# Three double bursts of attention instead of six single ones in a fused attention and feed-forward kernel

## The chip, the cores and the metric

The kernel runs on one core of one Trainium2 chip. The core has TensorE (PE in the profile; its weight loads are PEld), VectorE (DVE), ScalarE (ACT), GpSimd (POOL) and SyncE (SP), which work side by side and meet through semaphores; each carries out its own instructions in the order in which the program lists them. SP and POOL mostly issue DMAs. The metric is the device time of one execution in microseconds (us). Before the change its median over 3 runs is 819.44 us (819.32 to 822.13).

## The reference

Attention works in chunks: each row of 64 tokens of one head attends only to its own chunk. The result, laid out as 4608 tokens of 512 numbers, goes through a feed-forward pair of matrices with a quadratic relu between them. All of it is fp32.

```python
B, H, S, D = 8, 8, 576, 64
scores = (1 / sqrt(D)) * matmul(q_c, k_c.transpose(0, 1, 2, 4, 3))   # chunks of 64
scores = scores - max(scores, axis=-1, keepdims=True)
attn = exp(scores); attn = attn / (sum(attn, axis=-1, keepdims=True) + 1e-09)
x = matmul(attn, v_c)  # then to (B * S, H * D) = (4608, 512)
h = x @ w_in           # w_in (512, 2048)
g = where(h >= 1, h, where(h <= -1, 0, (h + 1) ** 2 / 4))
out = g @ w_out        # w_out (2048, 512)
```

## The kernel before

**Tiles and turns.** The 4608 tokens are nine tiles of 512 (`NTILE`). In each tile the eight heads are four pairs (`NP`), so that attention has 36 *turns*, one for each tile and pair; `turn` numbers them and `AT` gives tile and pair back. Tiles 0 to 2 (`ALONE`) are worked one at a time. Tiles 3 and 4, then 5 and 6, then 7 and 8 go together: for two tiles at once a scheme of seven block products (`P1` to `P7`, in the manner of Strassen) makes first h (the loop over `alternating(0, NQ)`, 56 products of six matmuls of 512 columns, in `product`, L903) and then the output (`both_out`, 56 products of twelve matmuls, L1119). Turns 20 to 27 are tiles 5 and 6, turns 28 to 35 tiles 7 and 8; turns of equal number modulo two share their buffers.

**A turn** is: the loads of q and k (`load_heads`, L382, four DMAs of 64 KB each, rows of 32 numbers, on SP) and of v (L398, two DMAs); two block transposes on DVE that make `qT` and `kT` (`attn_turn`, L441; one buffer of each); the scores, 32 matmuls of 64 columns (`scores_of`, L465); the softmax (`attn_softmax`: a maximum on DVE at L521, eight exponentials on ACT at L532, normalising on DVE at L550 to L556, a block transpose on DVE at L573, and eight DMAs at L565 that move the quarters into `aT`, four on SP and four on POOL); the values, 32 matmuls (`values_of`, L487); and a copy out of the bank on ACT (`keep_x`). Of `q_sb`, `k_sb`, `v_sb` and `aT` there are two buffers each. Scores and values of a turn go into the bank pair `ps_a`.

**Bursts.** While two tiles are in their h and output stages, the attention of the next two runs in between: `between` is called ahead of each product, and at the places of `BURSTS` (5, 14, 23, ... 68, counted over the 112 products of both stages) it calls `burst`, which puts on PE the values of turn n and the scores of turn n + 2 in one stretch. There are eight bursts in the stages of tiles 3 and 4 (for turns 20 to 27) and eight in those of tiles 5 and 6 (turns 28 to 35). Six of each eight lie in the h stage.

**The order.** Everything is added to a `Plan`, which writes the instructions out by a list schedule: a part goes to its engine when the plan's own costs say that it is ready, the earlier added first, with `ahead` moving a part's place. So the order on each engine is fixed when the program is built, and a change of a cost or a place can move instructions on all of them. POOL also issues the loads of the ring of ten factors (256 KB each) from which each product takes one (`from_ring`), and its share of the moves into `aT`.

**Temporaries and banks.** `tmp_bufs` are four buffers; in tiles 0 to 2 the weights are prepared and the output rows are staged in them (`store`, L671 for the DMAs of tile 2, issued on SP). From tile 3 on they are not used. The bank pair of `ps_o2` and `ps_o3` (`o_pair`) is used in the output stages and not in the h stages.

Of the kernel before, what the change touches and what calls it, by code (L numbers as in the profile page):

```python
# [133 lines left out]
def kernel(  # L134
# [38 lines left out]
    def turn(t, g):  # L173
        if t <= ALONE:
            return t * NP + g
        d, m = divmod(t - ALONE - 1, 2)
        return (ALONE + 1) * NP + d * 2 * NP + 2 * g + m

    AT = {turn(t, g): (t, g) for t in range(NTILE) for g in range(NP)}

    sb = ctx.enter_context(tc.tile_pool(name="sb", bufs=1))
# [75 lines left out]
    def room(name, bufs, t, g):  # L257
        if t == 0 and (name, g) in first:
            return first[name, g]
        if t > 0 and name in ("e", "x"):  # L260
            return wheel[(2 * turn(t, g) + (name == "x")) % 3]
        return bufs[turn(t, g) % len(bufs)]

# [208 lines left out]
    def values_of(t, g):  # L472


        akey, aT = room("aT", aT_bufs, t, g)
        vkey, v_sb = room("v", v_bufs, t, g)
        pkeys, pair = bank_pair_of(t, g)
        halves = aT.rearrange("p (e c q) -> p c e q", e=2, q=Q)

        def emit():  # L480
            for n in range(CT // 2):
                for h in range(2):
                    at = (2 * n + h) * C
                    of = h * HALF + n * C
                    for half in range(2):
                        rows = slice(half * C, (half + 1) * C)
                        nc.tensor.matmul(  # L487
                            out=pair[h * C:(h + 1) * C, half, HALF + n * C:HALF + (n + 1) * C],
                            lhsT=v_sb[rows, of:of + C],
                            rhs=aT[rows, at:at + C] if t == 0 else halves[rows, of // C],  # L490
                            start=True, stop=True,
                        )

        return emit, (f"{akey}_0", f"{akey}_1", vkey), pkeys

    def attn_products(*some, lag=0.0):

        plan.add(
            "pe", 0.2 + 0.6 * len(some), lambda: [emit() for emit, _, _ in some],
            [k for _, reads, _ in some for k in reads],  # L500
            [k for _, _, writes in some for k in writes],
            columns=1024 * len(some), lag=lag,
        )

    def bank_pair_of(t, g):
        if t == 0 and g % 2:
            return ("ps_o2", "ps_o3"), o_pair
        return ("ps_a0", "ps_a1"), a_pair

    def attn_softmax(t, g):  # L510
# [14 lines left out]
        if sums:  # L525
            plan.add("dve", 0.08, lambda: nc.vector.tensor_scalar_mul(mx, mx, -SCALE), (), (mkey,))  # L526

            many = 2 if t > ALONE else 1

# [52 lines left out]
    def attn_split(t, g):  # L582
        if t > ALONE:
            keep_x(t, g)
            return
        pkeys, pair = bank_pair_of(t, g)
        hkey, xh = xh_bufs[g][t % 2]
# [163 lines left out]
    def keep_x(t, g):  # L751
        i = g // 2
        pkeys, pair = bank_pair_of(t, g)
        name = "eo"[g % 2] + "BA"[(t - ALONE) % 2]
# [194 lines left out]
    LATER = -60  # L949
    BURSTS = range(5, 72, 9)  # L950
    sums = {
# [109 lines left out]
    def both_out(t, wide=(), then=None):  # L1061
# [123 lines left out]
        for name in OUT_ORDER:  # L1185
            taken["slots"] = 0 if name in some else taken["slots"]
            for p in range(NQ):
                between(len(alternating(0, NQ)) + NQ * OUT_ORDER.index(name) + p)
                if last and name == "P3" and p >= NQ - 2:
# [188 lines left out]

    def between(n):
        if n in BURSTS and turns:  # L1380
            burst(*turns.pop(0))

    turns = [(n, n + 2) for n in range((ALONE + 3) * NP, ALL - 2)] + [(ALL - 2, None), (ALL - 1, None)]
    for t in range(ALONE + 1, NTILE, 2):
        if t > ALONE + 1:
            move_blocks()
        for n, (p, name) in enumerate(alternating(0, NQ)):
            between(n)
            if t == ALONE + 1 and name == "P1":
# [72 lines left out]
```

## Time and profile before

| what | value |
|---|---|
| median of 3 runs | 819.44 us |
| the profiled execution | 821.0 us |
| its span, first to last instruction | 819.2 us |
| PE busy | 808.1 us (99%) |
| DVE busy | 659.2 us (80%) |
| ACT busy | 538.3 us (66%) |
| granted TensorE clock, mean of the span | 1.000 |
| DMA, moved in the span | 181.61 MB, mean 222 GB/s |

A busy PE row says that a matmul was under way, not that PE was at its peak: matmuls are pipelined, and what a product costs is best read from the distance between the starts of two products that follow each other. An instruction's own time can also overlap that of the next one on its engine. `x6` at the end of a timeline row means that six like instructions are merged into it.

### The profile page before, as it was taken

What the parts mean: (1) busy time and instruction counts of PE and PEld (TensorE: products, weight loads), DVE (VectorE), ACT (ScalarE), POOL (GpSimd) and SP (SyncE); (2) the same over time, 40 slices, a digit from 0 to 9 for tenths busy, and PEclk for the clock granted to TensorE, in tenths of its full rate; (3) what the DMA queues carried; (4) which work ended last, traced back from release to release, by engine and by line L of the source; (5) the groups of instructions that cost most, each with busy time, mean ns of one, the idle gap of its engine ahead of it and who ended that gap; (6) DMA issues with size and microseconds to landing.
All of it is one profiled execution on the core that took longest, in us unless ns stands there. A gap on an engine that the chain in (4) does not pass through costs nothing.

```text
span 819.2 us, 18533 instructions
## 1 busy us (share of the span) xinstructions
PE 808.1 (99%) x6464; PEld 694.7 (85%) x6464; DVE 659.2 (80%) x1143; ACT 538.3 (66%) x1295; POOL 343.2 (42%) x606
## 2 busy tenths in 40 slices
PE   8999999999999999999999999999999999999998
PEld 7888778878888888878899998878999988888887
DVE  4899997768799976887899875778995845589963
ACT  4799876455677675778985446878844456686450
POOL 2112223565655463546454333554433333333330
PEclk9999999999999999999999999999999999999999
DMA  9999725887998896999999678987676776667763
GB/s 205 260 266 309 176 47 142 252 276 220 285 260 231 209 276 155 299 270 285 257 244 267 183 232 245 246 232 219 193 201 183 227 220 196 192 190 192 213 200 110
DMA packets 245356, 181.61 MB, mean 222 GB/s; under 512 B 192656, under 2 KB 210576, under 8 KB 245264
## 3 DMA queue, kind: packets, MB, share of 16 engines
q0 software_dynamic: 40640, 122.72, 47.7%
q1 hardware_dynamic: 202512, 57.18, 30.6%
q8 instruction: 52, 0.85, 0.4%
q10 hardware_dynamic: 2112, 0.52, 0.3%
q14 instruction: 40, 0.33, 0.1%
HBM read 133.17 MB, written 38.80 MB: 210 GB/s over the span
## 4 chain that ended last, share of the span: by engine, by line
PE 86%; DMA 6%; DVE 3%; SPq 2%; ACT 1%; issue 1%; DVEq 0%; POOL 0%; ACTq 0%; POOLq 0%
PE ps_o L1119 19%; PE ps_h L610 14%; PE ps_o L646 13%; PE ps_h L903 13%; PE ps_o L903 13%; PE ps_h L1119 8%; PE ps_a L1119 3%; PE ps_a L487 2%; DMA words<-in_moe_w_in_dram 2%; PE ps_a L465 2%; DMA k_sb<-in_k_dram 1%; DMA aT<-e 1%; SPq L398 1%; DMA first<-in_q_dram 1%; DMA new_wo<-combos 1%
## 5 line engine op out<-in xcount | busy, mean ns | idle before, releaser
L728 ACT CAST new_wi<-new_wi 128x512 fp32r<-128x512 f32 x156 | 94.5, 625 | 63.8 <-PE ps_o L1119 32.1
L732 DVE TENSOR_TENSOR new_wi<-new_wi,new_wi 128x512 fp32r<-128x512 f32 (+2 forms) x194 | 124.8, 673 | 13.2 <-ACT new_wi L728 12.8
L610 PE MATMUL ps_h<-xh,parts 128*128 128x512 f32 x384 | 129.9, 397 | 1.7 <-DVE parts L350 1.2
L646 PE MATMUL ps_o<-parts,gh 128*128 128x512 f32 x384 | 118.4, 390 | 0.0
L610 PEld LDWEIGHTS ps_h<-xh,parts 128*128 128x128 f32 x384 | 71.9, 188 | 18.5 <-DVE parts L350 2.1
L565 POOL DMA_DIRECT2D aT<-e x96 | 48.5, 512 | 88.7 <-ACT tmp L323 34.3
L646 PEld LDWEIGHTS ps_o<-parts,gh 128*128 128x128 f32 x384 | 71.9, 188 | 15.0
L646 PE MATMUL ps_o<-parts,gl 128*128 128x512 f32 x192 | 74.7, 389 | 0.0
L934 DVE SCALAR_TENSOR_TENSOR new_wi<-h,new_wi 128x512 f32<-128x512 f32 x62 | 41.8, 685 | 30.7 <-ACT new_wi L933 30.0
L532 ACT ACTIVATE e<-ps_a,mx 128x64 f32<-128x64 f32 x168 | 50.8, 330 | 12.1 <-DVE mx L526 5.7
L933 ACT ACTIVATE new_wi<-new_wi 128x512 f32<-128x512 f32 x84 | 51.7, 639 | 0.9
L610 PE MATMUL ps_h<-x_parts,parts 128*128 128x512 f32 x128 | 50.0, 390 | 0.0
L930 ACT ACTIVATE new_wi<-h 128x512 f32<-128x512 f32 x62 | 38.9, 642 | 13.1 <-DVE h L924 12.8
L629 ACT CAST gh<-r 128x512 fp32r<-128x512 f32 x48 | 29.9, 622 | 26.6 <-DVE r L621 16.6
L646 PEld LDWEIGHTS ps_o<-parts,gl 128*128 128x128 f32 x192 | 36.0, 188 | 7.5
L621 DVE SCALAR_TENSOR_TENSOR r<-ps_h,r 128x512 f32<-128x512 f32 x48 | 32.6, 682 | 9.7 <-ACT r L620 9.7
L732 DVE TENSOR_TENSOR new_wi<-new_wi 128x512 f32<-128x512 f32 (+2 forms) x64 | 40.0, 631 | 0.5
L617 ACT ACTIVATE r<-ps_h 128x512 f32<-128x512 f32 x48 | 29.2, 608 | 14.9 <-PE ps_h L610 14.7
L532 ACT ACTIVATION_READ_ACCUMULATOR e<-ps_a,mx 128x1 f32 x168 | 37.3, 222 | 0.0
L631 DVE TENSOR_TENSOR gl<-r,gh 128x512 fp32r<-128x512 f32 x48 | 32.8, 684 | 4.0 <-ACT gh L629 3.2
L1119 PE MATMUL ps_o<-new_wo,new_wi 128*128 128x256 f32 (+1 forms) x244 | 35.0, 293 | 0.0
L1119 PE MATMUL ps_o<-ring_r,new_wi 128*128 128x256 f32 (+1 forms) x244 | 34.6, 292 | 0.0
(260 smaller groups left out, 2148.1 us busy)
## 6 DMA issues: line engine op xcount, KB each, us to landing
ring_r<-combos POOLq DMA_DIRECT2D x36, 256.0 KB, 3.5
new_wo<-sums_P POOLq DMA_DIRECT2D x36, 256.0 KB, 3.8
new_wi<-combos POOLq DMA_DIRECT2D x34, 256.0 KB, 4.2
new_wi<-sums_P POOLq DMA_DIRECT2D x34, 256.0 KB, 3.0
ring_gh<-combos POOLq DMA_DIRECT2D x33, 256.0 KB, 3.3
ring_gl<-combos POOLq DMA_DIRECT2D x33, 256.0 KB, 3.4
ring_gh<-sums_P POOLq DMA_DIRECT2D x33, 256.0 KB, 3.2
ring_gl<-sums_P POOLq DMA_DIRECT2D x33, 256.0 KB, 4.8
```

The costliest lines, as they stand in the source:

```text
L532: nc.scalar.activation(out=e3[:, n, :], in_=sc[:, n // 4, n % 4, :], func=AF.Exp, bias=mx[:, n, :], scale=SCALE, accum_out=sm[:, n, :],)
L565: queues[queue].dma_start(out=aT[b:b + Q, to], in_=x[a:a + Q, of])
L610: nc.tensor.matmul(out=ps, lhsT=weight["wi", j][:, half, kc * P:(kc + 1) * P], rhs=x, start=(kc == 0 and i == 0), stop=(kc == KC - 1 and i ...
L631: plan.add("dve", 0.6, lambda: nc.vector.tensor_tensor(out=gl, in0=now(r), in1=gh.bitcast(F32), op=ALU.subtract), (rkey, ghkey), (glkey,), ...
L646: nc.tensor.matmul(out=acc, lhsT=x[:, cols], rhs=weight["wo", j][:, half, :], start=(j == 0 and i == 0), stop=(j == NF - 1 and i == 2),)
L728: "act", cost, lambda: nc.scalar.copy(out=out(), in_=src()), reads, writes, ahead=ahead
L732: plan.add("dve", cost, lambda: nc.vector.tensor_tensor(out=out(), in0=one(), in1=two(), op=op), reads, writes, port=True, ahead=ahead)
L903: nc.tensor.matmul(out=ps, lhsT=w()[:, at:at + P], rhs=y(), start=name in FRESH and i == 0 and k == 0, stop=i == 1 and k == 2, skip_group_ ...
L930: plan.add("act", 0.52, lambda: nc.scalar.activation(out=now(r), in_=h(), func=AF.Relu, bias=0.5, scale=0.5), (hkey,), (rkey,), ahead=50)
L933: plan.add("act", 0.52, lambda: nc.scalar.square(out=now(r), in_=now(r)), (), (rkey,), ahead=50)
L934: plan.add("dve", 0.6, lambda: nc.vector.scalar_tensor_tensor(out=now(r), in0=h(), scalar=1.0, in1=now(r), op0=ALU.max, op1=ALU.min), (hke ...
L1119: nc.tensor.matmul(out=into, lhsT=x()[:, block], rhs=factor, start=first and k == 0, stop=p == NQ - 1 and k == len(steps) - 1, skip_group_ ...
```

## The change

In the h stages of tiles 3 to 6 the six bursts become three with two turns each, at the places 8, 25 and 43 of `BURSTS`, which now holds the number of turns for each place; the two bursts in the output stage stay at 59 and 68 with one turn each. A double burst has four groups of 32 matmuls: values of n and n + 1, then scores of n + 2 and n + 3. The second turn's values and scores go into the pair `ps_o2`, `ps_o3` (the set `beside`). From turn 23 (`TWOS` is 22) the odd turns' `qT` and `kT` are the first two of `tmp_bufs`, so that two turns' operands can stand ready at once; the transposes of turn 23 are added ahead of the h stage. A part with four groups has a lower cost in the plan than two parts with two. For all turns above tile 2 the eight exponentials of a turn are four parts of two instead of two parts of four.

```diff
+    TWOS = (ALONE + 3) * NP + 2
@@ room
+        if name in ("qT", "kT") and turn(t, g) >= TWOS and turn(t, g) % 2:
+            return tmp_bufs[name == "kT"]
@@ attn_products
-            "pe", 0.2 + 0.6 * len(some), lambda: [emit() for emit, _, _ in some],
+            "pe", 0.2 + 0.6 * len(some) if len(some) < 3 else 0.57 + 0.46 * len(some), lambda: ...
@@
-    def bank_pair_of(t, g):
-        if t == 0 and g % 2:
+    beside = set()
+
+    def bank_pair_of(t, g, what="scores"):
+        if (t == 0 and g % 2) or (what, turn(t, g)) in beside:
             return ("ps_o2", "ps_o3"), o_pair
@@ attn_softmax
-            many = 2 if t > ALONE else 1
+            many = 4 if t > ALONE else 1
@@
-    BURSTS = range(5, 72, 9)
+    BURSTS = {8: 2, 25: 2, 43: 2, 59: 1, 68: 1}
@@
-    def between(n):
-        if n in BURSTS and turns:
-            burst(*turns.pop(0))
+    def burst_of(ns):
+        ms = [n + 2 for n in ns if n + 2 < ALL]
+        if len(ns) == 2:
+            beside.update((("values", ns[1]), ("scores", ns[1] + 2)))
+        attn_products(
+            *(values_of(*AT[n]) for n in ns), *(scores_of(*AT[m]) for m in ms), lag=0.8
+        )
+        for m in ms:
+            attn_softmax(*AT[m])
+        for n in ns:
+            attn_split(*AT[n])
+        for m in ms:
+            if m + 2 < ALL:
+                load_heads(*AT[m + 2], "qk")
+        for n in ns:
+            if n + 2 < ALL:
+                load_heads(*AT[n + 2], "v")
+        for m in ms:
+            if m + 2 < ALL:
+                attn_turn(*AT[m + 2])
+
+    def between(t, n):
+        many = BURSTS.get(n, 0)
+        if many and turns:
+            burst_of([turns.pop(0) for _ in range(many)])
...
+    attn_turn(*AT[TWOS + 1])
```

On SP, from the last stores of tile 2's rows (`out_0_dram<-tmp`) on, the order before is this. `v_sb`, `q_sb`, `k_sb` are loads, `aT` the moves of a turn's probabilities; the digit behind a name is the buffer, 0 for even turns and 1 for odd ones.

```order
L671 DMA out_0_dram<-tmp0_135 64x512 x2
L398 DMA v_sb0_72<-in_v_dram 128x4x64 x2
L382 DMA q_sb1_69<-in_q_dram 32x16x32 x4
L382 DMA k_sb1_71<-in_k_dram 32x16x32 x4
L565 DMA aT0_78<-e0_76 32x256 x4
L398 DMA v_sb1_73<-in_v_dram 128x4x64 x2
L382 DMA q_sb0_68<-in_q_dram 32x16x32 x4
L382 DMA k_sb0_70<-in_k_dram 32x16x32 x4
L565 DMA aT1_79<-x0_80 32x256 x4
```

And this it is with the change, from the same stores to the moves that the second double burst needs.

```order
L676 DMA out_0_dram<-tmp0_135 64x512 x2
L385 DMA k_sb1_71<-in_k_dram 32x16x32 x4
L385 DMA q_sb1_69<-in_q_dram 32x16x32 x4
L401 DMA v_sb0_72<-in_v_dram 128x4x64 x2
L401 DMA v_sb1_73<-in_v_dram 128x4x64 x2
L385 DMA q_sb0_68<-in_q_dram 32x16x32 x4
L385 DMA k_sb0_70<-in_k_dram 32x16x32 x4
L385 DMA q_sb1_69<-in_q_dram 32x16x32 x4
L385 DMA k_sb1_71<-in_k_dram 32x16x32 x4
L570 DMA aT0_78<-e0_76 32x256 x4
L570 DMA aT1_79<-x0_80 32x256 x4
```

Before, one turn's loads of q and k stand between the loads of v and a turn's moves; now two turns' loads stand there, and both turns' moves come behind them.

On DVE, at the start of the h stage of tiles 3 and 4, the order before is this (`STREAM_TRANSPOSE` at L441 makes `qT` and `kT`, `TENSOR_REDUCE` at L521 is the maximum of the first burst's scores, the rows on `h`, `parts` and `new_wi` belong to h and to the factors).

```order
L924 TENSOR_TENSOR h_3626<-ps_h1_142,snaps_3638 128x512
L934 SCALAR_TENSOR_TENSOR new_wi9_10_3337<-h_3626,new_wi9_10_3337 128x512
L732 TENSOR_TENSOR new_wi0_0_2553<-parts_15_1359 128x512
L732 TENSOR_TENSOR new_wi1_1_2619<-parts_16_1420 128x512
L732 TENSOR_TENSOR new_wi1_1_2619<-new_wi0_0_2553 128x256
L732 TENSOR_TENSOR new_wi0_0_2553<-new_wi0_0_2553,new_wi1_1_2619 128x256
L732 TENSOR_TENSOR new_wi0_0_2553<-new_wi0_0_2553 128x256
L732 TENSOR_TENSOR new_wi1_1_2619<-new_wi1_1_2619,new_wi0_0_2553 128x256
L521 TENSOR_REDUCE mx0_81<-ps_a_138 128x8
L441 STREAM_TRANSPOSE qT0_74<-q_sb1_69 128x512
```

With the change the same place reads as follows; the two rows of L444 that write `tmp0` are turn 23's `kT` and `qT` (`tmp0` is the tile of the first two temporaries).

```order
L929 TENSOR_TENSOR h_3626<-ps_h1_142,snaps_3638 128x512
L444 STREAM_TRANSPOSE tmp0_135<-k_sb1_71 128x512
L939 SCALAR_TENSOR_TENSOR new_wi9_10_3267<-h_3626,new_wi9_10_3267 128x512
L737 TENSOR_TENSOR new_wi0_0_2552<-parts_15_1359 128x512
L444 STREAM_TRANSPOSE tmp0_135<-q_sb1_69 128x512
L737 TENSOR_TENSOR new_wi1_1_2619<-parts_16_1420 128x512
L737 TENSOR_TENSOR new_wi1_1_2619<-new_wi0_0_2552 128x256
L737 TENSOR_TENSOR new_wi0_0_2552<-new_wi0_0_2552,new_wi1_1_2619 128x256
L737 TENSOR_TENSOR new_wi0_0_2552<-new_wi0_0_2552 128x256
L929 TENSOR_TENSOR h_3626<-ps_h1_142,h_3626 128x512
```

The two transposes have moved in among the first operations of the h stage, into buffers from which the stores of tile 2 are sent, and the first maximum, eight rows behind the first row shown before, now stands sixteen rows behind it (eleven behind the second transpose).

## Rows read from the trace of the kernel before

**Rows 1.** The page: span, and busy time by engine.
```profile
span 819.2 us, 18533 instructions
PE 808.1 (99%) x6464; PEld 694.7 (85%) x6464; DVE 659.2 (80%) x1143; ACT 538.3 (66%) x1295; POOL 343.2 (42%) x606
```

**Rows 2.** Stretches of tiles 3 and 4: PE, PEld, DVE, ACT, POOL, PEclk, DMA, GB/s.
```profile
340.00:356.00 16.00, 15.71 (x138) 12.34 (x140) 12.60 (x23) 11.23 (x33) 10.13 (x20) 1.00 1.09 295
356.00:372.00 16.00, 15.91 (x130) 13.12 (x122) 14.27 (x28) 13.76 (x37) 7.67 (x15) 1.00 1.05 272
```

**Rows 3.** Waits of PE, 324 to 415: total, times, longest.
```profile
PE ps_o L903 <- DVE h L924: 0.3, 1, 0.3
```

**Rows 4.** Timeline of PE around bursts: start, us, instruction.
```profile
330.70 0.69 PE L487 MATMUL ps_a<-aT,v_sb 64*64 64x64 f32 x32
...
337.39 1.52 PE L903 MATMUL ps_o<-new_wi,ring_gl 128*128 128x512 f32 x6
338.75 1.52 PE L903 MATMUL ps_o<-new_wi,new_wo 128*128 128x512 f32 x6
340.21 0.69 PE L487 MATMUL ps_a<-aT,v_sb 64*64 64x64 f32 x32
340.72 0.65 PE L465 MATMUL ps_a<-kT,qT 64*64 64x64 f32 x32
341.33 0.98 PE L903 MATMUL ps_h<-xl,new_wo 128*128 128x512 f32 x3
342.15 0.86 PE L903 MATMUL ps_h<-new_wi,new_wo 128*128 128x512 f32 x3
342.84 1.55 PE L903 MATMUL ps_o<-new_wi,new_wi 128*128 128x512 f32 x6
```

**Rows 5.** Timeline of SP's queue, h stage of tiles 3 and 4.
```profile
323.94 5.07 SPq L671 DMA_DIRECT2D out_dram<-tmp  x8
...
333.97 3.30 SPq L382 DMA_DIRECT2D q_sb<-in_q_dram  x4
337.37 3.33 SPq L382 DMA_DIRECT2D k_sb<-in_k_dram  x4
340.80 3.06 SPq L565 DMA_DIRECT2D aT<-e  x4
...
346.25 3.48 SPq L382 DMA_DIRECT2D q_sb<-in_q_dram  x4
349.82 4.33 SPq L382 DMA_DIRECT2D k_sb<-in_k_dram  x4
...
376.11 2.74 SPq L382 DMA_DIRECT2D q_sb<-in_q_dram  x4
378.95 6.03 SPq L382 DMA_DIRECT2D k_sb<-in_k_dram  x4
385.08 3.38 SPq L565 DMA_DIRECT2D aT<-e  x4
```

**Rows 6.** DMA issues, 325 to 405: KB each, median us to landing.
```profile
q_sb<-in_q_dram SPq DMA_DIRECT2D x23, 64.0 KB, 5.8
out_dram<-tmp SPq DMA_DIRECT2D x7, 128.0 KB, 5.3
aT<-e SPq DMA_DIRECT2D x12, 32.0 KB, 5.0
```

**Rows 7.** Timeline of DVE behind a burst.
```profile
374.78 0.68 DVE L521 TENSOR_REDUCE mx<-ps_a 128x8 f32<-128x512 f32 x1
375.38 0.70 DVE L441 STREAM_TRANSPOSE qT<-q_sb 128x512 f32<-128x512 f32 x1
```

**Rows 8.** Timeline of SP's queue, h stage of tiles 5 and 6.
```profile
502.59 1.92 SPq L382 DMA_DIRECT2D q_sb<-in_q_dram  x4
504.61 3.06 SPq L382 DMA_DIRECT2D k_sb<-in_k_dram  x4
511.61 2.86 SPq L565 DMA_DIRECT2D aT<-e  x4
```

More of the change, by code (lines that the diff above doesn't have):

```diff
@@ L476, in values_of @@
         vkey, v_sb = room("v", v_bufs, t, g)
-        pkeys, pair = bank_pair_of(t, g)
+        pkeys, pair = bank_pair_of(t, g, "values")
         halves = aT.rearrange("p (e c q) -> p c e q", e=2, q=Q)
@@ L498, in attn_products @@
         plan.add(
-            "pe", 0.2 + 0.6 * len(some), lambda: [emit() for emit, _, _ in some],
+            "pe", 0.2 + 0.6 * len(some) if len(some) < 3 else 0.57 + 0.46 * len(some), lambda: [emit() for emit, _, _ in some],
             [k for _, reads, _ in some for k in reads],
@@ L585, in attn_split @@
             return
-        pkeys, pair = bank_pair_of(t, g)
+        pkeys, pair = bank_pair_of(t, g, "values")
         hkey, xh = xh_bufs[g][t % 2]
@@ L752, in keep_x @@
         i = g // 2
-        pkeys, pair = bank_pair_of(t, g)
+        pkeys, pair = bank_pair_of(t, g, "values")
         name = "eo"[g % 2] + "BA"[(t - ALONE) % 2]
@@ L1187, in both_out @@
             for p in range(NQ):
-                between(len(alternating(0, NQ)) + NQ * OUT_ORDER.index(name) + p)
+                between(t, len(alternating(0, NQ)) + NQ * OUT_ORDER.index(name) + p)
                 if last and name == "P3" and p >= NQ - 2:
@@ L1377 @@
         take(f"ring_{key}", key, [P, T], F32R, (key,), (f"ring_{key}",))
-    def between(n):
-        if n in BURSTS and turns:
-            burst(*turns.pop(0))
-    turns = [(n, n + 2) for n in range((ALONE + 3) * NP, ALL - 2)] + [(ALL - 2, None), (ALL - 1, None)]
+    def burst_of(ns):
[22 more added lines that the diff above has]
+            burst_of([turns.pop(0) for _ in range(many)])
+    turns = list(range((ALONE + 3) * NP, ALL))
+    attn_turn(*AT[TWOS + 1])
     for t in range(ALONE + 1, NTILE, 2):
@@ L1387 @@
         for n, (p, name) in enumerate(alternating(0, NQ)):
-            between(n)
+            between(t, n)
             if t == ALONE + 1 and name == "P1":
```

## The prediction

> **What bounds the kernel now.** I read the page first: PE is busy for 808.1 of 819.2 us [rows 1], so that only what PE issues, or what makes it wait, moves the time. Next the stretches of the h stage of tiles 3 and 4: beside a full PE, DVE is busy for 12.6 of 16 and 14.3 of 16 us, ACT for 11.2 and 13.8, and the DMA engines have no room at all, with shares of 1.09 and 1.05 [rows 2]. Then PE's waits from 324 to 415 us: one of 0.3 us [rows 3]. So the h stage runs at PE's pace, with three other resources close behind it. Last the timelines of PE around a burst and of SP, which carries the loads of q, k and v and half of the moves into `aT`, to see what a burst costs and how early its operands come. The granted clock is 1.00 in both stretches, bursts included [rows 2], and I take it to stay.
>
> **A, the saving on PE.** Products follow each other at 1.36 us (337.39 to 338.75); the next would start at 340.11. The burst's first group starts at 340.21, its second at 340.72, the product behind at 341.33, and the one behind that at 342.84 [rows 4]. So a burst costs 342.84 - 340.11 - 1.36 = 1.37 us: two groups of 0.51 and 0.35 for the change-over at both ends. A double burst costs 4 x 0.51 + 0.35 = 2.39 against 2 x 1.37 = 2.74. There are six of them in tiles 3 to 6: 6 x 0.35 = 2.1 us less. This is certain, and it is all that can be gained, as PE waits for nothing else there [rows 3].
>
> **B, the first double burst.** It needs turn 23's `qT` and `kT`, which now go into temporaries. Tile 2's four results rotate over the same buffers, so the last pair of stores reads the one for `qT`. The eight stores are issued from 323.94 for 5.07 us, the last from about 328.4 [rows 5]; landing takes 5.3 [rows 6]: the buffer is free at 333.7 and its transpose done at 334.4 (0.7) [rows 7]. By PE the burst could start two products after the first single one, at 330.70 + 2.72 = 333.4 [rows 4]. It starts at 334.5: 1.1 us late (0 if the stores land early, 3 if late). DVE stands in its queue at that transpose, with eleven rows between it and the first maximum in the new order: this is what makes the next term larger.
>
> **C, the second double burst.** This decides. In the new order SP issues, behind the loads of v, four groups of q and k loads, and only then the moves of turns 22 and 23, which the burst's values need. The q of turn 26 can only be loaded when DVE has transposed that of turn 24. From 334.4 DVE has ten rows of 0.6 (start to start) [rows 7], four half as wide (taken as 0.4) and a small one ahead of that transpose, 7.7 us; the transpose itself ends at 342.8. In the trace a pair of q and k takes 333.97 to 340.80 = 6.8 us and 346.25 to 354.15 = 7.9 at this place, 8.9 later (376.11 to 384.98) [rows 5], and 5.1 in tiles 5 and 6 (502.59 to 507.67) [rows 8]. I take the mean of the two nearest, 7.35. Two pairs end at 342.8 + 14.7 = 357.5; two groups of moves at 3.06 to 3.38, together 6.4 [rows 5], end at 363.9; the last one, issued 0.8 earlier, lands 5.0 after its issue [rows 6], at 368.1. PE is there at 334.5 + 2.39 + 18 x 1.36 = 361.4 (the order has 18 products between the two bursts). So PE stands for 6.7 us.
>
> The bounds: at 5.1 for a pair and moves at 2.86 [rows 8] the moves land at 342.8 + 10.2 + 5.7 + 4.2 = 362.9, 1.5 late; if in addition DVE has no backlog and the loads start 2.1 us behind the burst, as at 333.97 behind the single one, C is nothing. At 8.9 and 3.38 it is 342.8 + 17.8 + 6.8 + 4.2 - 361.4 = 10.2.
>
> In the old order two turns overlapped: while one turn's moves landed, the other's loads were issued, and the moves went out at 340.80, behind one pair [rows 5]. Now SP has nothing left to issue while the last moves land, and the pause cannot be made up.
>
> Two rules of the Trainium skill bear on C. The DMA share of 1.09 [rows 2] says that loads by SP and the ring's loads by POOL take from one store; the Trainium skill (Trainium Kernel Development and Optimization, Key Constraints) says that DMAs from SP, ACT and POOL all run on the same 16 engines and interleave. By it the slow pairs of this stage hold for four groups in a row, where the fast pair of the other stage would make the sum +0.5 instead of +7.6. The moves of 32 KB land after 5.0 us [rows 6]; the Trainium skill (DMA: Bandwidth & Descriptors, Anatomy of one DMA) puts a DMA's fixed time at about 2.0 us. An estimate by that page has each late burst 3.0 us earlier and the sum at +2.7; the trace differs from it here, and I go by the trace.
>
> **D and E, the third double burst and the next single one.** The first maxima stand directly behind the second burst in the new order, so q's load starts 2.1 (the burst) + 2.5 (four DVE rows) = 4.6 us after its start. For the third burst three groups come ahead of the moves: 4.6 + 11.0 + 6.4 + 4.2 = 26.2 against 2.39 + 17 x 1.36 = 25.5: 0.7. For the single burst that follows 17 products later, four groups but one turn's moves: 4.6 + 14.7 + 3.2 + 4.2 = 26.7 against 25.5: 1.2. Bounds: nothing (pairs at 5.1), and 3.1 and 4.3 (at 8.9).
>
> **F, tiles 5 and 6.** Pairs at 5.1 and moves at 2.86: 4.6 + 10.2 + 5.7 + 4.2 = 24.7 against 26.9: nothing late. Later bursts there have no q and k to load.
>
> **The rest.** Exponentials in four parts: the same instructions, no change; PE's single wait of 0.3 bounds the gain, and I allow as much for a loss. POOL's moves have ring loads queued behind them; the new order has 23 ring loads ahead of turn 23's moves, so product 24 can be late only where the burst is late anyway. The banks `ps_o2` and `ps_o3` are next written 14 products after the third double burst: no wait.
>
> **The sum.** -2.1 + 1.1 + 6.7 + 0.7 + 1.2 = +7.6 us. On the profiled execution, 821.0 us (1.8 of it outside the span of 819.2), that is 828.6; it was 1.6 above the median of the runs, and on the median of 819.44 it is 827.0.
>
> **Rivals.** *The loads keep up:* not slower. Place: the second double burst. With p us for a pair C is 2p - 8.0, and below p = 6.7 D and E are nothing; so the sum is -2.1 + 1.1 + 2p - 8.0, and it decides at p = 6.5, where it reaches the 4.1 us (0.5%) that a measurement of this kernel can tell from no change. Price: at the pairs and moves of tiles 5 and 6 the sum is +0.5, 819.9; without B's backlog and wait it is -2.1, 817.3. For it: those pairs [rows 8], and a ring that fills up while PE stands still and then leaves the engines to SP. Against: none of the pairs shown from tiles 3 and 4 was faster than 6.8 [rows 5].
>
> *The softmax is late too:* sixteen exponentials and two turns' DVE work fall on engines that are busy for 11 to 14 of 16 us [rows 2]. A single turn's moves went out 8.9 us after its scores' end (330.70 + 0.51 + 0.65 = 331.9 to 340.80) [rows 4, 5]. The second turn has 25.5 - 2.1 - 3.2 - 4.2 = 16.0 us before the third double burst is late by it, 17.4 before the second. At twice the single turn's time, 17.8, the third double burst in tiles 3 and 4 is late by 1.8 instead of 0.7, and in tiles 5 and 6 the second by 0.4 and the third by 1.8: the sum is +10.9, 830.3. For it: ACT and DVE alternate in a turn and both are fuller than before. Against: the second turn's work starts beside the first's, and both had 2 to 5 us of every 16 free.
>
> *A gain of over 0.5%* would need more than the 2.1 of A; no wait of PE is there to give it.
>
> *The bursts don't come out double:* excluded by the order, which has them behind 7, 25 and 42 products.
>
> **How the numbers follow.** Slower as summed, with C between 3 and 10, 823.5 to 832: 0.48. The softmax late too, up to 836: 0.12. The loads keep up, within 0.5% (815.3 to 823.5): 0.36. Faster by over 0.5%: 0.04. The range from 817 to 834 reaches down to the case in which nothing is late (817.3); above, it leaves out the one in which B, C, D and E all stand at their upper ends, 819.4 - 2.1 + 3 + 10.2 + 3.1 + 4.3 = 838. The summed case by itself has 823.5 to 832.
>
> **What the changed profile would show.** For A: four groups of 0.51 between products, 2.4 us in all. For B: a transpose into `tmp` on DVE that waits for a store, and a first double burst that starts 1 us late. For C: SP issuing q and k until about 357 and moves until 364, and PE idle for several us ahead of the second double burst, released by a DMA into `aT`. I am wrong if that gap is under 2 us, if the wait is for DVE or ACT instead, or if tiles 5 and 6 have the larger gap.

## The result and the profile after

The changed kernel takes 827.63 us in the median of 6 runs (825.98 to 829.85), beside 821.11 (819.32 to 822.68) for the kernel before on the same chips: a ratio of 1.0086, with a 95% interval from 1.0073 to 1.0098. It is slower by 6.5 us by the medians and 7.1 by the ratio. The predicted time was 827.0, 7.6 us above the 819.44 of the first three runs.

The page of the profiled execution (826.45 us), against [rows 1]:

```profile
span 824.7 us, 18516 instructions
...
PE 809.8 (98%) x6464; PEld 697.9 (85%) x6464; DVE 658.6 (80%) x1143; ACT 536.6 (65%) x1295; POOL 342.9 (42%) x606
```

The work is the same; the span is 5.5 us longer. Counting matmuls in both traces gives where: the changed kernel is 1.56 us ahead when h of tiles 3 and 4 begins (up to there the change is in the parts of the exponentials alone; other kernels with the same parts, below, stood between 1.6 ahead and 1.4 behind, so this is not the change's), loses 8.14 in that stage, nothing in the output stage, and wins 1.12 in h of tiles 5 and 6. The waits of PE from 324 to 430 us (in all, times, longest), against [rows 3]:

```profile
PE ps_o L490 <- DMA aT<-x: 1.8, 1, 1.8
PE ps_o L908 <- ACT snaps L733: 1.7, 1, 1.7
PE ps_a L490 <- DMA aT<-x: 1.1, 1, 1.1
PE ps_o L908 <- DVE h L929: 0.9, 1, 0.9
PE ps_h L908 <- DVE h L929: 0.7, 1, 0.7
```

They add up to 6.2 us where there were 0.3. PE's timeline around the three double bursts (start, us, instruction, and in brackets the idle time before it with what ended it), against [rows 4]:

```profile
331.86 0.69 PE L490 MATMUL ps_a<-aT,v_sb 64*64 64x64 f32 x32
...
334.80 1.65 PE L908 MATMUL ps_h<-new_wi,ring_gl 128*128 128x512 f32 x6 [0.68 <-DVE h L929]
...
342.27 1.65 PE L908 MATMUL ps_o<-new_wi,new_wi 128*128 128x512 f32 x6 [1.74 <-ACT snaps L733]
...
360.20 1.52 PE L908 MATMUL ps_o<-new_wi,ring_r 128*128 128x512 f32 x6
362.83 0.92 PE L490 MATMUL ps_a<-aT,v_sb 64*64 64x64 f32 x32 [1.11 <-DMA aT<-x]
365.60 1.25 PE L490 MATMUL ps_o<-aT,v_sb 64*64 64x64 f32 x29 [1.84 <-DMA aT<-x]
...
371.31 1.56 PE L908 MATMUL ps_o<-new_wi,ring_gh 128*128 128x512 f32 x6
...
380.57 0.96 PE L908 MATMUL ps_o<-xl,ring_r 128*128 128x512 f32 x3 [0.89 <-DVE h L929]
...
392.97 0.84 PE L908 MATMUL ps_h<-xl,new_wo 128*128 128x512 f32 x3
...
394.43 0.69 PE L490 MATMUL ps_a<-aT,v_sb 64*64 64x64 f32 x32
394.94 0.75 PE L490 MATMUL ps_o<-aT,v_sb 64*64 64x64 f32 x29
...
398.10 1.54 PE L908 MATMUL ps_o<-new_wi,new_wi 128*128 128x512 f32 x6
```

At the second double burst the product behind it should start at 360.20 + 1.36 + 2.39 = 363.95 and the next at 365.31; that one starts at 371.31, 6.0 us late. Only 2.95 of it is idle time. Most of the rest is the clock, which the windows show (columns as in [rows 2]; PEclk is the third figure from the end):

```profile
340.00:356.00 16.00, 14.26 (x63) 11.32 (x62) 13.17 (x26) 14.59 (x51) 8.15 (x16) 1.00 1.07 274
356.00:372.00 16.00, 13.04 (x163) 10.79 (x162) 11.04 (x21) 7.52 (x14) 5.80 (x12) 0.79 0.83 234
364.50:371.30 6.80, 5.70 (x102) 5.05 (x103) 3.36 (x8) 1.76 (x4) 0.69 (x1) 0.50 0.63 183
```

From 364.5 to 371.3 us the granted clock is 0.50, the lower level of 1.2 GHz. Three groups and a product took 371.31 - 365.60 = 5.71 us; at the third double burst, at full clock, the same took 398.10 - 394.94 = 3.16. So the half clock cost 2.55 us. By the trace's record of the clock it begins at 364.49, inside PE's second wait (363.76 to 365.60).

SP's queue in h of tiles 3 and 4, and in the last two rows of tiles 5 and 6, against [rows 5, 8]:

```profile
340.87 2.42 SPq L385 DMA_DIRECT2D q_sb<-in_q_dram  x4
343.39 5.91 SPq L385 DMA_DIRECT2D k_sb<-in_k_dram  x4
349.40 4.18 SPq L385 DMA_DIRECT2D q_sb<-in_q_dram  x4
353.68 2.25 SPq L385 DMA_DIRECT2D k_sb<-in_k_dram  x4
356.03 2.45 SPq L570 DMA_DIRECT2D aT<-e  x4
358.60 2.69 SPq L570 DMA_DIRECT2D aT<-x  x4
...
370.73 1.93 SPq L385 DMA_DIRECT2D q_sb<-in_q_dram  x4
372.76 2.73 SPq L385 DMA_DIRECT2D k_sb<-in_k_dram  x4
...
380.66 7.51 SPq L570 DMA_DIRECT2D aT<-e  x8
...
514.52 1.92 SPq L385 DMA_DIRECT2D q_sb<-in_q_dram  x4
516.54 2.71 SPq L385 DMA_DIRECT2D k_sb<-in_k_dram  x4
```

Four groups of loads stand ahead of the moves, as forecast. The DMA issues from 325 to 405 us (KB each, median us to landing), against [rows 6]:

```profile
aT<-e SPq DMA_DIRECT2D x12, 32.0 KB, 4.7
...
aT<-x SPq DMA_DIRECT2D x4, 32.0 KB, 4.3
```

And on DVE, against [rows 7], the transpose into a temporary waits for tile 2's stores:

```profile
331.73 0.71 DVE L444 STREAM_TRANSPOSE tmp<-q_sb 128x512 f32<-128x512 f32 x1 [2.75 <-DMA out_dram<-tmp]
```

### The profile page after: what moved, and what is told of

It reads as the page before. It is cut to its first block, busy times and chain, and to the rows that moved or that the text cites. A ratio compares the mean times of both kernels' runs of the same rounds, so it can differ in the third digit from the quotient of the medians.

```text
span 824.7 us, 18516 instructions
## 1 busy us (share of the span) xinstructions
PE 809.8 (98%) x6464; PEld 697.9 (85%) x6464; DVE 658.6 (80%) x1143; ACT 536.6 (65%) x1295; POOL 342.9 (42%) x606
## 4 chain that ended last, share of the span: by engine, by line
PE 88%; DMA 6%; DVE 2%; SPq 2%; ACT 1%; issue 1%; ACTq 0%; DVEq 0%; POOL 0%
PE ps_o L1124 19%; PE ps_h L615 14%; PE ps_o L651 14%; PE ps_o L908 13%; PE ps_h L908 12%; PE ps_h L1124 8%; PE ps_a L1124 3%; DMA words<-in_moe_w_in_dram 2%; PE ps_a L490 2%; PE ps_a L468 2%; DMA k_sb<-in_k_dram 1%; DMA out_dram<-tmp 1%; DMA first<-in_q_dram 1%; DMA aT<-x 1%; SPq L385 1%
## 5 line engine op out<-in xcount | busy, mean ns | idle before, releaser
L733 ACT CAST new_wi<-new_wi 128x512 fp32r<-128x512 f32 x156 | 97.0, 634 | 70.0 <-PE ps_o L1124 31.2
L737 DVE TENSOR_TENSOR new_wi<-new_wi,new_wi 128x512 fp32r<-128x512 f32 (+2 forms) x194 | 124.6, 672 | 15.2 <-ACT new_wi L733 14.7
L939 DVE SCALAR_TENSOR_TENSOR new_wi<-h,new_wi 128x512 f32<-128x512 f32 x62 | 42.3, 685 | 31.6 <-ACT new_wi L938 31.5
L537 ACT ACTIVATE e<-ps_a,mx 128x64 f32<-128x64 f32 x136 | 41.8, 328 | 10.3 <-DVE mx L531 4.8
L626 DVE SCALAR_TENSOR_TENSOR r<-ps_h,r 128x512 f32<-128x512 f32 x48 | 32.8, 683 | 12.7 <-ACT r L625 12.6
L622 ACT ACTIVATE r<-ps_h 128x512 f32<-128x512 f32 x48 | 29.1, 606 | 16.3 <-PE ps_h L615 16.2
L636 DVE TENSOR_TENSOR gl<-r,gh 128x512 fp32r<-128x512 f32 x48 | 32.8, 684 | 4.8 <-ACT gh L634 3.9
L570 POOL DMA_DIRECT2D aT<-x x48 | 24.3, 513 | 24.8 <-DVE r L626 7.7
```

The lines of the kernel that those rows point to most:

```text
L537: nc.scalar.activation(out=e3[:, n, :], in_=sc[:, n // 4, n % 4, :], func=AF.Exp, bias=mx[:, n, :], scale=SCALE, accum_out=sm[:, n, :],)
L570: queues[queue].dma_start(out=aT[b:b + Q, to], in_=x[a:a + Q, of])
L626: plan.add("dve", 0.6, lambda: nc.vector.scalar_tensor_tensor(out=r, in0=ps, scalar=1.0, in1=r, op0=ALU.max, op1=ALU.min), (pkey,), (rkey,))
L733: "act", cost, lambda: nc.scalar.copy(out=out(), in_=src()), reads, writes, ahead=ahead
L737: plan.add("dve", cost, lambda: nc.vector.tensor_tensor(out=out(), in0=one(), in1=two(), op=op), reads, writes, port=True, ahead=ahead)
L939: plan.add("dve", 0.6, lambda: nc.vector.scalar_tensor_tensor(out=now(r), in0=h(), scalar=1.0, in1=now(r), op0=ALU.max, op1=ALU.min), (hke ...
```

## The experiments

Each kernel ran in 5 rounds beside the kernel before, whose median was 820.94 us for the first four, 821.28 for the next four and 820.79 for the last two. Unless said otherwise an edit is made to the changed kernel. What a stage loses or wins is counted, as above, by the matmuls of the one profiled execution against those of the kernel before.

**1. The other temporaries** (`e1_tmp12`): is B the wait for one store?

```diff
-            return tmp_bufs[name == "kT"]
+            return tmp_bufs[1 + (name == "kT")]
```

> The change, but the odd turns' qT and kT go into the second and third temporary, which tile 2's first two stores free, instead of the first, which its last store frees. Theory (the transpose behind the last store holds DVE up, and through DVE and ACT holds PE up): DVE's wait of 2.75 us for a store goes, and with it PE's two waits of 0.7 and 1.7 us behind the first double burst; loads and moves also come about 2.4 us earlier, so the wait ahead of the second double burst stays near 3 us. About 2.4 us less than the changed kernel, 825. Rival (PE's two waits come from the double softmax itself, on DVE and ACT): they stay, and the time stays at 827.6. Rival (SP's loads alone set the second burst's time): PE gets there 2.4 us earlier and waits 5.4 us instead, 827.6.

Measured: 830.02 us, 1.0105 [1.0091, 1.0118]; I had expected 825. The wait did not go: DVE stood 2.57 us at the transpose of k instead of q, since the stores read these buffers too. Of PE's two waits behind the first burst (332.44) one is gone and the other shrank from 1.74 to 1.10, so that PE came to the second burst 28.8 us after the first instead of 29.9. But the moves landed at 369.52, 37.1 us after the first burst's start instead of 33.7, and PE waited longer for them:

```profile
364.21 1.36 PE L490 MATMUL ps_a<-aT,v_sb 64*64 64x64 f32 x32 [2.99 <-DMA aT<-e]
369.52 1.41 PE L490 MATMUL ps_o<-aT,v_sb 64*64 64x64 f32 x29 [3.95 <-DMA aT<-x]
```

SP's first pair of loads took 11.8 us here (340.72 to 352.55), against 8.4 in the changed kernel (340.87 to 349.30). So SP's queue sets the second burst's time; 1.1 us of the longer wait is PE coming earlier, and most of it the slower queue. On B the run settles nothing.

**2. Without two loads of k** (`e2_no_k`): k of turns 26 and 27 is not loaded, and their scores use the k that lies there.

```diff
-            if n not in which:
+            if n not in which or (n == "k" and t > 0 and turn(t, g) in (26, 27)):
```

> The change, with the loads of k for turns 26 and 27 left out (these two turns are computed with older k). SP has two groups of loads fewer ahead of the moves for the second double burst, about 7 us by the changed kernel's trace; all else is alike. Theory (SP's queue of loads makes the moves late): the moves of turn 23 go out when their data is ready, at about 353, land at about 360, and PE, which is there at 361.6, waits for nothing; with the idle time the fall of the clock to half goes too: 5 to 6 us less than the changed kernel, 822. Rival (the second turn's softmax is late): the wait of about 3 us and the fall of the clock stay, 827. Rival (a double burst makes the clock fall by itself): the wait goes, the clock falls as before, 824.5.

Measured: 824.81 us, 1.0048 [1.0034, 1.0062]; I had expected 822. On SP the moves come 4.9 us earlier than in the changed kernel and find the second burst on time (SP's queue, then PE):

```profile
342.28 7.89 SPq L385 DMA_DIRECT2D q_sb<-in_q_dram  x8
351.17 2.65 SPq L570 DMA_DIRECT2D aT<-e  x4
354.47 2.41 SPq L570 DMA_DIRECT2D aT<-x  x4
```

```profile
363.04 0.69 PE L490 MATMUL ps_a<-aT,v_sb 64*64 64x64 f32 x32
363.55 0.75 PE L490 MATMUL ps_o<-aT,v_sb 64*64 64x64 f32 x29
```

No wait for `aT`, and the clock stays at 1.0. What is left in this stage are waits of 0.8, 1.7 and 1.5 us for DVE and ACT. This shows C: the loads ahead of the moves; since the DMA engines also have less to carry here, queue and engines are told apart by experiment 10 only. The total missed by 2.8 us. The stage loses 3.6 us instead of 8.1, so that 4.5 are won where 5.5 of idle time and half clock had gone, and 0.6 went into a longer wait for DVE (1.48 us at 376.86); why the runs won only 2.8 stays open.

**3. Work instead of a wait** (`e3_fill`): 20 matmuls of 512 columns into the idle bank `ps_o2`, ahead of the second double burst.

```diff
+                for _ in range(20):
+                    nc.tensor.matmul(out=o_pair[:, 0, :], lhsT=fill()[:, :P], rhs=fill(), start=True, stop=True)
+                emit()
```

> The change, with 20 matmuls of 512 columns (0.227 us each, 4.5 us) ahead of the second double burst, into a bank that is free there, so that PE works while the moves land. Theory (the clock falls because PE stands idle, in two waits of 1.1 and 1.8 us around the burst's first group): the clock stays at 1.00 from 364 to 371, the burst takes 2.4 us instead of 3.0 for its last three groups, the product behind it 1.4 instead of 2.7; the fill ends at about 366.2, 0.6 later than the last wait, so the time is 1.5 to 2 us under the changed kernel's, 826. Rival (small matmuls of attention let the clock fall): it falls all the same, and the time is 0.6 to 1 us over the changed kernel's.

Measured: 828.78 us, 1.0093 [1.0079, 1.0108], not below the changed kernel's 827.63; I had expected 826. The burst runs at full clock now, 368.74 to 370.98, but the fill took 4.6 us, and the stage loses 8.0 us, as good as the 8.1 of the changed kernel. So a PE that is kept at work keeps its clock with the same double burst behind it; as a remedy the fill is worth nothing.

**4. The exponentials alone** (`e4_parts`): the kernel before with four parts.

```diff
-            many = 2 if t > ALONE else 1
+            many = 4 if t > ALONE else 1
```

> The kernel before, with the exponentials of turns above tile 2 in four parts of two instead of two of four, and nothing else of the change. In the changed kernel's one profile PE is 1.6 us ahead of the kernel before where the h stage of tiles 3 and 4 begins; 0.9 of it arose in the first 50 us, which this edit doesn't touch. Theory (0.9 is a matter of the single execution, and 0.7 comes with the finer parts): 0 to 0.7 us less than before, 818.7 to 819.4 against 819.4. Rival (finer parts cost, since exponentials and h now alternate on ACT): up to 1 us more.

Measured: 820.55 us, 0.9994 [0.9983, 1.0004]. This part of the change costs and gives nothing that the runs can tell, as costed. In its trace, whose bursts are all single, the h stage of tiles 5 and 6 is 0.54 us shorter than before.

**5. Moves ahead of the loads** (`e5_moves_first`): a load of q or k waits, in the plan, for the softmax of the burst's last turn.

```diff
-                load_heads(*AT[m + 2], "qk")
+                load_heads(*AT[m + 2], "qk", needs=(room("x", x_bufs, *AT[ms[-1]])[0],))
```

> The changed kernel, in which the loads of the next q and k wait in the plan for the softmax of the second turn of a burst, so that on SP's queue the moves of the weights (aT) stand ahead of four loads and not behind them; the planner then also sets the second burst seven products of h later. Theory (the order on SP's queue makes the moves late): they are issued at about 350 to 356 us and land by 362, no wait for aT and no half clock, and the loads, now from 356 on, still come in time for the bursts, which stand later too: 821 to 823 us, as for the kernel with spread bursts. Rival (loads and moves together fill SP's queue, so whichever stands last is late): the moves are in time and q and k are not; TensorE waits for a transposed q or k at the second or third burst, 2 to 6 us: 824 to 828.

Measured: 854.79 us, 1.0407 [1.0391, 1.0423]; I had expected 821 to 823. The moves were in time (issued from 351.50, no wait for `aT`), but SP had stood idle for 14.4 us ahead of them (337.09 to 351.50), the four loads then lasted to 372.73, and PE waited at the second burst for a transpose instead, and behind it for DVE and ACT, whose work had piled up:

```profile
PE ps_h L908 <- DVE h L929: 3.5, 2, 3.4
PE ps_o L468 <- DVE tmp L444: 3.0, 1, 3.0
PE ps_h L908 <- DVE new_wi L939: 2.3, 1, 2.3
PE ps_o L908 <- ACT h L733: 2.2, 1, 2.2
```

The rival named the wait, but neither its reason nor its size: 20.9 us are lost in tiles 3 and 4 and 13.6 in tiles 5 and 6, where PE waits for DVE and ACT. The edit itself kept SP idle until the second turn's softmax was done. So the run does not show that the queue is full, nor what another order on a busy queue would give; it shows that these loads cannot wait for the softmax.

**6. Doubles in tiles 5 and 6 alone** (`e6_late_only`): the kernel before up to the end of tiles 3 and 4.

```diff
-    TWOS = (ALONE + 3) * NP + 2
+    TWOS = (ALONE + 5) * NP + 2
@@ between
+        if t == ALONE + 1:
+            if n in range(5, 72, 9):
+                m = turns.pop(0)
+                burst(m, m + 2)
+            return
```

> The kernel before, with double bursts in the h of tiles 5 and 6 alone; in the h of tiles 3 and 4 the bursts stay single and nine products apart. Theory (three double bursts are worth 0.35 us each, and in the h of tiles 5 and 6 nothing is late, as the changed kernel's gain of 1.1 us there shows): 1 us below the kernel before, 819.9 us against 820.9, a ratio of 0.9987. Rival (the 1.1 us there is the giving back of what was lost earlier, since transfers and buffers had more time): no gain, 820.5 to 821.5.

Measured: 820.41 us, 0.9988 [0.9979, 0.9997]: 0.9 us below before by the medians and 1.0 by the ratio (0.2 to 1.7 by its interval), as expected. PE waits for nothing in the h stage of tiles 3 and 4 here, so there is no earlier loss to be given back. But the trace does not show three doubles at 0.35: the second of them waits 0.47 us for `aT`, and the stage is 0.30 us shorter than before, where experiment 4's single bursts had it 0.54 shorter. How much of the 1.0 us is due to the doubles stays open.

**7. Spread bursts** (`e8_spaced`): more products between the double bursts.

```diff
-    BURSTS = {8: 2, 25: 2, 43: 2, 59: 1, 68: 1}
+    BURSTS = {8: 2, 30: 2, 48: 2, 66: 1, 76: 1}
```

> The changed kernel with its bursts spread out: the second double burst five products of h later (30 products of h ahead of it instead of 25), the third seven later, the two single ones seven and eight output places later. Nothing is added or removed. Theory (the second burst comes before its moved weights, which SP's queue delivers 33.7 us after the first burst's start, and the half clock follows from that wait): the burst now comes some 36 us after the first, the two waits for aT (1.1 and 1.8 us) are gone, the granted clock stays at 1.0, and of the loss only the 2.4 us behind the vector engine's wait for the store are left, less 0.35 for each double burst: 821.5 us, between 820 and 823, against 821 before and 827.6 changed. Rival (the queue and the engines have no room for bursts of twice the size, wherever they stand: the moves are as late as the burst): a wait for aT of 1 to 3 us stays, and the time with it, 825 to 828. Second rival (the half clock comes from the small matmuls of a double burst and not from the wait): a stretch at half clock of about 7 us stays without a wait, 824 us.

Measured: 833.53 us, 1.0152 [1.0133, 1.0170], a miss by 12. The second burst did what was expected, 36.4 us after the first (334.83), without a wait and at clock 1.00; its four groups are no cause of the half clock. But the third came 28.4 us after the second:

```profile
371.23 0.69 PE L490 MATMUL ps_a<-aT,v_sb 64*64 64x64 f32 x32
...
399.61 0.69 PE L490 MATMUL ps_a<-aT,v_sb 64*64 64x64 f32 x32
404.62 1.25 PE L490 MATMUL ps_o<-aT,v_sb 64*64 64x64 f32 x29 [4.32 <-DMA aT<-e]
```

Its moves landed 33.4 us after the burst before; the last of them stood behind four loads of 3.75, 4.91, 4.09 and 2.32 us. So the first rival came true, one burst later: the wait went to the third burst, with its half clock, and the third burst's softmax fell into the start of the output stage, where PE waited 1.0 and 1.2 us more. I had set the third burst's distance by the changed kernel, in which 28.8 us were enough (365.60, the second group of the second burst, to 394.43; from its first group, as counted here, it is 31.6); there the pair of loads behind PE's pause had taken only 4.8 us (370.73 to 375.49), in and just after a stretch with a DMA share of 0.63.

**8. Spread bursts, later transposes** (`e7_both`): as 7, with the bursts again two to three places later, and the planner's landing time for tile 2's stores raised, so that the two transposes into temporaries move back.

```diff
-        plan.add("sp", 0.6, send, (okey,), (), lag=4.0, moving=0.8)
+        plan.add("sp", 0.6, send, (okey,), (), lag=8.0 if t == ALONE else 4.0, moving=0.8)
@@
-    BURSTS = {8: 2, 25: 2, 43: 2, 59: 1, 68: 1}
+    BURSTS = {8: 2, 33: 2, 51: 2, 68: 1, 78: 1}
```

> As the kernel with spread bursts (e8_spaced), and the planner is told that the stores of tile 2 land 8 us after their issue instead of 4, so that VectorE transposes the q and k of turn 23 into the temporaries some instructions later (the first burst moves two products of h later; the second stands 32 products in, the third 49). Theory (the 2.75 us stand of VectorE at the transpose that waits for the store is what reaches TensorE as 0.7 and 1.7 us): the transposes no longer wait, both waits behind the first burst go, and with six double bursts at 0.35 us each the time falls below that before: 819 us, between 818 and 820.5. Rival (those two waits are ScalarE's and VectorE's own load at the start of h, whatever the transposes do): they stay, 821 to 822 us.

Measured: 829.59 us, 1.0110 [1.0085, 1.0134]. The part on B came out: the transposes (333.08 and 335.23 us) wait for nothing, and both waits behind the first burst (0.7 and 1.7) are gone. The total, expected at 819, missed, again by the third burst: it begins 26.1 us after the second (397.15 after 371.03), PE waits 2.25 us in it for `aT`, and later 2.5 us for ACT's exponentials at the start of the output stage. The stage loses 8.2 us. The places hold for tiles 5 and 6 too, and there PE waits 2.5 us for the exponentials once more (588.96); 4.0 us more are lost in those stages.

**9. Two doubles, then singles** (`e9_two_doubles`): distances of 23 products between the doubles and 21 to the next single burst in tiles 3 and 4; landing time of the stores as in 8.

```diff
+    BURSTS = {
+        ALONE + 1: {8: 2, 33: 2, 53: 1, 62: 1, 71: 1, 80: 1},
+        ALONE + 3: {8: 2, 25: 2, 43: 2, 59: 1, 68: 1},
+    }
```

> Two double bursts in the h of tiles 3 and 4, 9 and 32 products in, then four single ones (the first 21 products after the second double burst), with the planner told that the stores of tile 2 land after 8 us; in the h of tiles 5 and 6 three double bursts as in the changed kernel. Theory (in the h of tiles 3 and 4 the moved weights of a double burst land 33.4 to 33.7 us after the start of the burst before, and that alone makes the next one late): 23 products and a burst are some 34 us, and the single bursts come when the weights of their turn are long there; nothing waits over 0.5 us, the clock stays at 1.0, and five double bursts give 5 x 0.35 = 1.75 us: 819.4 us against 821.1 before, between 818.5 and 820.3. Rival (a double burst in the h of tiles 3 and 4 costs something wherever it stands, by its softmax on ScalarE and VectorE in one lump): waits of TensorE for ScalarE or VectorE of 1 us and more in sum after the doubles, 820.5 to 823.

Measured: 819.43 us, 0.9975 [0.9963, 0.9988], 2.0 us below before by the ratio and 1.4 by the medians (expected 1.75). Both doubles and the single burst behind them find their operands:

```profile
336.85 0.69 PE L490 MATMUL ps_a<-aT,v_sb 64*64 64x64 f32 x32
...
348.60 1.65 PE L908 MATMUL ps_o<-new_wi,ring_r 128*128 128x512 f32 x6 [0.92 <-DVE h L929]
...
372.33 0.69 PE L490 MATMUL ps_a<-aT,v_sb 64*64 64x64 f32 x32
...
403.39 0.69 PE L490 MATMUL ps_a<-aT,v_sb 64*64 64x64 f32 x32
```

The 0.92 us is PE's one wait from 300 to 700 us. It takes what the two doubles save: the h stage of tiles 3 and 4 is as long as before, and that of tiles 5 and 6 is 1.07 us shorter. So the trace accounts for 1.1 us of the 2.0; it is of one of the slower executions (820.63, of 816.37 to 821.05), and what the faster ones save no trace shows. This version beats the kernel before and the changed one; that it beats number 6 the intervals don't show.

**10. All moves by POOL** (`e10_pool_moves`): those of turns 22 to 25 that stood on SP.

```diff
-                queue = "pool" if t == 1 or j else "sp"
+                queue = "pool" if t == 1 or j or turn(t, g) in range(TWOS, TWOS + 4) else "sp"
```

> The changed kernel, in which the moves of the weights of turns 22 to 25 that stand on SP's queue are issued by POOL, which issues the other half already; the planner sets the second burst one product of h later. Theory (the four loads ahead of the moves on SP's queue make them late, not the DMA engines): all moves are issued by 358 us, on the heels of the transposes at 349 and 352.3 us, and land by 363, when TensorE comes; a wait of at most 1 us is left, the clock does not fall, and the time is 822.5 us, between 821.3 and 824 (the wait for the store stays, and the third burst may be up to 2 us late, since its moves have POOL's weight loads before them). Rival (the 16 DMA engines are full in this stretch, so a move lands at the same time whichever queue issues it): moves land at 365 to 366, waits and half clock as in the changed kernel, 826 to 828.

Measured: 833.36 us, 1.0144 [1.0127, 1.0160]; I had expected 822.5. At the place that the edit touches the theory held: the last move was issued by 360.76 and PE began the second burst at 363.26 without a wait, at clock 1.00. The rival, that the DMA engines make the move late whoever issues it, is refuted there: the four loads took as long as in the changed kernel (340.75 to 355.42, against 340.87 to 355.93). The third burst, 25.6 us after the second, found its moves in time as well. But the first single burst, whose moves are on SP again, stood behind four loads (395.37 to 413.49):

```profile
388.88 0.69 PE L490 MATMUL ps_a<-aT,v_sb 64*64 64x64 f32 x32
...
421.65 1.25 PE L490 MATMUL ps_a<-aT,v_sb 64*64 64x64 f32 x29 [6.88 <-DMA aT<-x]
```

Here the moves land 32.8 us after the double burst before.

Put together, by the start of a double burst and what follows it in tiles 3 and 4:

| kernel, next burst | PE there after | moves landed after | wait |
|---|---|---|---|
| changed, second double | 29.9 us | 33.7 us | 1.1 + 1.8 us |
| changed, third double | 31.6 | in time | 0 |
| other temporaries (1), second double | 28.8 | 37.1 | 3.0 + 3.9 |
| without two loads (2), second double | 29.9 | in time | 0 |
| fill (3), third double | 26.9 | in time | 0 |
| spread (7), second double | 36.4 | in time | 0 |
| spread (7), third double | 28.4 | 33.4 | 4.3 |
| spread, later (8), second double | 34.0 | in time | 0 |
| spread, later (8), third double | 26.1 | 29.1 | 2.3 |
| by POOL (10), second double | 31.5 | in time | 0 |
| by POOL (10), third double | 25.6 | in time | 0 |
| by POOL (10), first single | 25.9 | 32.8 | 6.9 |
| two doubles (9), second double | 35.5 | in time | 0 |
| two doubles (9), first single | 31.1 | in time | 0 |

There is no one distance that is enough: moves that came late landed 29 to 37 us after the burst before, while SP's moves were in time for a burst after 26.9 us in experiment 3. The 33.4 to 33.7 us that the expectation of experiment 9 builds on were two cases.

## Why the prediction was right

**A held in kind with its size too high, and F held.** The third double burst cost 398.10 - (392.97 + 1.36) - 1.36 = 2.41 us, against 2.39. But a single burst costs less than the 1.37 us read at 340.21. At 526.66 in the trace before, the product ahead of it and the second one behind it are

```profile
525.21 1.52 PE L903 MATMUL ps_h<-new_wi,ring_r 128*128 128x512 f32 x6
...
529.25 1.52 PE L903 MATMUL ps_o<-new_wi,ring_gh 128*128 128x512 f32 x6
```

so it cost 529.25 - 525.21 - 2 x 1.36 = 1.32 us, and ten of the twelve single bursts cost 1.32 or 1.33 when they are counted like this. The three doubles of tiles 5 and 6 cost 2.25, 2.42 and 2.42, which saves 0.83 us and not 1.05: "this is certain" was too strong for 0.35 each. In tiles 5 and 6 the pair of loads took 4.73 us (514.52 to 519.25), no wait came, and the stage won 1.12 us. What it won beyond 0.83 lies between the bursts and is not the doubles'; experiment 4 won 0.54 there without them.

**B had the cause and not the path.** DVE did stand at the transpose into a temporary, for 2.75 us, but the first burst was not late: scores of turn 23 are the last of its four groups. The step that failed is "it starts at 334.5: 1.1 us late". DVE's stand reached PE behind the burst, as 0.68 + 1.74 = 2.42 us. In experiments 8 and 9, with the transposes further back, neither wait is there; the burst stands two products later in them too, which was not separated.

**C held in place, order and lateness of the moves, and not in what the lateness is made of.** Two pairs of loads took 15.1 us (340.87 to 355.93) where 14.7 were forecast, two groups of moves 5.3 where 6.4; the moves landed 33.7 us after the first burst's start, against 33.6. PE came 3.0 us later than reckoned (29.9 after the first burst's start, not 26.9), 2.4 of it by B, and had one group to do within the wait, so the idle time was 2.95 us and not 6.7. Most of the missing part came from a cost that the prediction had excluded with "the granted clock is 1.00 ... and I take it to stay": 2.55 us. With 0.5 more, which stands around the group that ran between the two waits, that is 6.0. Experiment 2 shows that the loads on SP's queue are the cause, 10 that at this burst it is the queue and not the DMA engines behind it.

On the two rules weighed there: the Trainium skill (DMA: Bandwidth & Descriptors, Anatomy of one DMA) puts a DMA's fixed time at about 2.0 us, for DMAs that GpSimd issues. Here the moves of 32 KB land after 4.7 and 4.3 us on SP's queue, and after 3.6 and 4.5 us on POOL's in the same view, so the trace differs and the sum by the page, +2.7, came out too low. The Trainium skill (the same page, Rules for kernel authors) says that issuing from several engines gives no bandwidth and only saves the issuing sequencer's time. In experiment 10 just that time was what was short, at the burst that the edit touches.

**D and E did not come:** no wait at the third double burst nor at the next single one, where 0.7 and 1.2 us were forecast. In D it was PE's time that failed, more than the loads'. The second burst, unbroken, would have begun at 365.60 - 0.51 = 365.09; the moves for the third landed 25.4 us behind that (390.50 in the trace), where 26.2 were forecast, but PE came 29.3 us behind it and not 25.5, held up by the half clock (2.55) and by DVE (0.89 at 380.57). In E it was the loads, taken as on a full queue: four groups took 11.1 us (400.31 to 411.40), not 14.7. In experiment 3 they took 13.5 (401.50 to 415.03), and the single burst did wait, 0.89 us. Of the softmax rival, 0.9 us at 380.57 (DVE) may be a trace, in the wrong place for it.

**The sum** for h of tiles 3 and 4 was -1.05 + 1.1 + 6.7 + 0.7 + 1.2 = 8.65 and is -1.05 + 2.42 + 6.0 + 0.89 = 8.26 by these rows (A's term left as forecast), 8.14 by the count of matmuls. That the total is so near is in part luck: the clock's 2.55 and B's 1.3 more with 1.4 of small ones stand for 3.75 less of idle time in C and 1.9 less in D and E. That the time itself, 827.63 us, lies only 0.6 from the forecast is luck as well: the difference was 6.5 us by the medians against 7.6, and the kernel before stood at 821.11 instead of 819.44.

## What to carry to other kernels

Work that is done in larger lumps needs its transfers in larger lumps too: add up what stands on the issuing queue between two lumps, and set the distance of the lumps by that, before counting the gain on the engine that computes. A later lump (experiments 7 and 8), or one lump's moves on another queue (10), handed the wait to the next lump; what helped, by 1 to 2 us, was to lump where the queue has time (6 and 9). When one engine is held up, look for the price at the products behind, not only at the instruction that waits.

## What the runs showed of the hardware

Once up, and ahead of the kernels' ends, the clock of TensorE fell to the lower level (0.50) only inside a pause of PE or within 1.6 us behind one. In the changed kernel it did so for 6.83 us from 364.49, inside the second of two waits (1.11 and 1.84 us, with one group of small matmuls between them); in experiment 1 for 10.24 us from 363.19, inside a wait of 2.99; in experiment 10 for 10.24 us from 417.28, inside a wait of 6.88; in experiment 7 for 3.41 us from 404.73, behind a wait of 4.32. In experiments 5 and 8 it fell three times each, for 3.41 us, in or behind waits of 2.25 to 3.39 us; the fall at 418.09 in experiment 8 came behind a wait of 2.52 us between large products, so that the small matmuls of a burst are not needed for it. Far from any change it fell in experiment 3 (from 7.66, behind a wait of 2.38) and in experiment 9 (from 43.09, behind one of 1.88), for 3.41 us each.

Waits without a fall were those of up to 1.74 us that stood alone, and three in experiment 5, of 2.18, 2.33 and 2.38 us; so these traces do not tell which waits of about 2 us bring a fall. In experiments 2 and 3 the clock stayed at 1.00 through the second double burst. In the changed kernel 2.95 us of waiting cost another 2.55 by the clock.
